# TensorE's transposes of gathered rows and of h's second half, set between the two groups of twelve second-layer products

## The chip, the cores and the metric

The kernel runs on one core of a Trainium2 chip. The metric is the device time of the program in microseconds (us), the median of three runs.

## What is computed

Attention over blocks of 64 positions (a query sees its own block and all before it), and then a mixture of experts that sends each token to one expert:

```python
# q, k, v: (8, 8, 576, 64);  w_gate: (512, 8);  w1: (8, 512, 1024);  w2: (8, 1024, 512)
scores = where(pos_i // 64 >= pos_j // 64, (q @ k.T) / 8, -1e9)
x = (softmax(scores) @ v)                    # reshaped to (4608, 512)
probs = softmax(x @ w_gate);  expert = argmax(x @ w_gate)
for e in range(8):
    mask = expert == e
    out[mask] = probs[mask, e] * (relu(x[mask] @ w1[e]) @ w2[e])
```

## The kernel before

Attention (class `Attention`) and routing (class `Router`) fill the first 372 us or so. Each token's row x is written to memory, and a table is built that lists the tokens of each expert in groups of 128, the tiles. The change concerns class `Experts`, which runs after that: 38 tiles, one after the other, each with its expert's weights.

Every product is made of three, since a float32 operand is split in a high and a low part: high times high, low times high, high times low. For one tile t:

- `gather(t)`: GpSimd issues an indirect DMA that fetches 128 rows into `xg`, two periods ahead.
- `rows_in(t)` (line 895): four TensorE transposes of `xg` into the bank `px`. `rows_act(t)` (lines 905 and 908): ScalarE copies it out twice, as the high part `xh` and whole as `xf`. `rows_pool(t)` (line 914): GpSimd makes the low part `xl` as their difference.
- `first_pe(t)` (line 936): 24 matmuls with w1; the halves f = 0 and 1 of the 1024 hidden values stand in two banks (`ph`, and one that the profile calls `o`). It starts with xh and needs xl from its fifth matmul on.
- The hidden values are transposed in two ways. Half 0: `planes` (line 983, ScalarE) takes `ph` apart in planes of 16 bits, `turned` (line 995) has the DMA transpose them from `h[0]` into `hf`, `joined` (line 1001) puts them together, and `joined_high` (lines 1009, 1010) applies the relu for the high part `hh` and for the whole. Half 1: `relu_act` (line 974), then `hidden_pe` (line 1018), four TensorE transposes into the bank `pt`, and `hidden_act` (lines 1028, 1031), two copies out of it.
- `hidden_low` (line 1037): GpSimd makes the low part `hl` of either half.
- `second_pe(t, part)` (line 1057): 24 matmuls with w2 into one bank, twelve in part 0 and twelve in part 1. Part 0 needs the high parts, and hl from its ninth matmul on.
- `out_act(t)` (line 1074) scales by the gate's weight, and `out_pool(t)` (line 1081) issues the DMA that scatters the rows.

The order on each engine is the order in which `period(t)` calls these; engines meet through semaphores. One call of `period(t)` holds the first layer of tile t, the rows of tile t + 1 and the second layer of tile t - 1. Some of the waits:

- `rows_act(t + 1)` waits for the rows' transposes, ScalarE's queue being strictly in this order;
- `hidden_pe(t, 1)` waits for both of ScalarE's steps that read the first layer's banks (`planes` and `relu_act(t, 1)`);
- `planes(t + 1)` writes `h[0]`, so it waits for the `hidden_low` of tile t that reads it; `relu_act` is behind it on ScalarE;
- `first_pe(t + 1)` waits for xh and, four matmuls on, for xl.

The weights of an expert (4 MB) come in eight DMAs issued by SyncE into five buffers (line 1176), and VectorE splits them (lines 1183, 1189) into one of two places, while the expert before is worked on. The first three tiles are special: their rows are fetched during attention, `begin()` handles tiles 0 and 1, and `period(2)` has the second layer of tile 0 and, before, another order.

Of the kernel before, what the change touches and what calls it, by code (L numbers as in the profile page):

```python
# [792 lines left out]
class Experts:  # L793
# [52 lines left out]
    def run(self):  # L846
# [37 lines left out]
        def gathered(t):  # L884

            return len([k for k in range(EARLY, t + 1) if k % 4 == t % 4])

        def rows_in(t):

            if t >= EARLY:  # L890
                pe.wait_ge(sg[t % 4], 16 * gathered(t))
            if t >= 2:
                pe.wait_ge(sem["xa"], 2 * t - 2)
            for k in range(4):
                m = pe.transpose(self.px[:, P * k : P * k + P], self.xg[t % 4][:, P * k : P * k + P], self.ident)
                if t == 1 and k < 2:

                    m.then_inc(sem[("mm1", "mm2")[k]], (3, 1)[k])
            m.then_inc(sem["xt"], 1)

        def rows_act(t):
            act.wait_ge(sem["xt"], t)
            if t >= 2:
                act.wait_ge(sem["mm1"], 2 * t + 1)
            act.copy(self.xh, self.px).then_inc(sem["xa"], 1)  # L905
            if t >= 2:
                act.wait_ge(sem["xp"], t - 1)
            act.copy(self.xf, self.px).then_inc(sem["xa"], 1)  # L908
# [59 lines left out]
        def relu_act(t, f):  # L968
            act.wait_ge(sem["mm1"], 2 * t + f + 2)
            if t == 2:  # L970
                act.wait_ge(sem["ht"], 4)
            elif t > 2:
                act.wait_ge(sem["hp"], 2 * t - 1)
            act.activation(self.h[f], self.ph[f], AF.Relu).then_inc(sem["ra"], 1)  # L974

        def planes(t):

            act.wait_ge(sem["mm1"], 2 * t + 2)
            if t == 2:
                act.wait_ge(sem["ht"], 3)  # L980
            else:
                act.wait_ge(sem["hp"], 2 * t)
            act.copy(  # L983
                self.h[0].bitcast(U16).rearrange("p (o c) -> p o c", o=2),
                self.ph[0].bitcast(U16).rearrange("p (c o) -> p o c", o=2),
            ).then_inc(sem["ra"], 1)

        def turned(t):

            if t == 2:  # L990
                act.wait_ge(sem["hp"], 4)
            else:
                act.wait_ge(sem["jo"], t - 2)
            act.wait_ge(sem["ra"], 2 * t - 1)
            act.dma_start_transpose(  # L995
                self.hf.bitcast(U16).rearrange("p (k c) -> p k c", c=P), self.h[0].bitcast(U16)
            ).then_inc(sem["tr"], 16)
# [14 lines left out]
        def hidden_pe(t, f):  # L1012
            if t:
                pe.wait_ge(sem["ra"], 2 * t + f - 1)
                pe.wait_ge(sem["ha"], 2 + 2 * f if t == 1 else 8 if t == 2 else 4 * t - 2)
            h = self.h[f] if t else self.xg[3 * f]
            for k in range(4):
                m = pe.transpose(self.pt[f][:, P * k : P * k + P], h[:, P * k : P * k + P], self.ident)  # L1018
            m.then_inc(sem["ht"], 1)

        def hidden_act(t, f):
            if t == 0 and f == 0:
                act.wait_ge(sem["lr"], 1)
                act.wait_ge(sem["lc"], 1)
            act.wait_ge(sem["ht"], 2 * t + f + 1 if t < 2 else t + 3)
            if t >= 2:
                act.wait_ge(sem["mm2"], t)
            act.copy(self.hh[t % 2][:, f], self.pt[f]).then_inc(sem["ha"], 1)
            if 0 < 2 * t + f < 4:
                act.wait_ge(sem["hp"], 2 * t + f)  # L1030
            act.copy(self.hf if t < 2 else self.h[f], self.pt[f]).then_inc(sem["ha"], 1)
# [7 lines left out]
        def second_pe(t, part):  # L1039
            e8, off = self.regs[t]  # L1040
            todo = [
                (h[t % 2], base, c) for h, base in ((self.hh, 8192), (self.hl, 8192), (self.hh, 12288)) for c in range(8)
            ]
            if part == 0:
                pe.wait_ge(sem["wh"], e8 + 8 if t >= EARLY else 4)
                pe.wait_ge(sem["ha"], 4 * t + 3)
                if t >= 2:
                    pe.wait_ge(sem["ya"], t - 1)
            for n in range(12 * part, 12 * part + 12):
                h, base, c = todo[n]  # L1050
                if n == 8:
                    pe.wait_ge(sem["hp"], 2 * t + 2)
                if t == 0 and n >= 16 and c % 2 == 0:
                    pe.wait_ge(sem["wd"], 5 + c // 2)
                elif n == 16:
                    pe.wait_ge(sem["wd"], e8 + 8)
                m = pe.matmul(  # L1057
                    self.py[t % 2],
                    h[:, c // 4, P * (c % 4) : P * (c % 4) + P],
                    wf[:, bass.ds(off + (base + 512 * c), 512)],  # L1060
                    start=n == 0,
                    stop=n == 23,
                )
            if part == 1:
                m.then_inc(sem["mm2"], 1)

        def out_act(t):
            act.wait_ge(sem["mm2"], t + 2)
            if t >= 1:
                act.wait_ge(sy, 16 * t)  # L1070
            else:

                act.wait_ge(sem["ga"], 48)
            act.activation(self.y, self.py[t % 2], AF.Copy, scale=self.xg[t % 4][:, GATE : GATE + 1]).then_inc(  # L1074
                sem["ya"], 1
            )
# [35 lines left out]
        def period(t):  # L1112
            more = t + 1 < NS
            if t > 2:
                first_pe(t)
                out_act(t - 2)
            planes(t)
            turned(t)
            relu_act(t, 1)
            if t == 2:  # L1120

                for f in range(2):
                    second_pe(0, f)
                out_act(0)
            elif more:
                rows_in(t + 1)
                rows_act(t + 1)
            hidden_pe(t, 1)
            hidden_act(t, 1)
            joined(t)  # L1130
            joined_high(t)
            for f in range(2):
                second_pe(t - 1, f)
                if t == 2 and f == 0:
                    rows_in(t + 1)
                    rows_act(t + 1)
            out_pool(t - 2)
            if t + 2 < NS:
                gather(t + 2)
            if more:  # L1140
                rows_pool(t + 1)
            for f in (1, 0):
                hidden_low(t, f, pool)
# [18 lines left out]
        with tc.tile_critical():  # L1162
# [94 lines left out]
            for t in range(2, least):  # L1257
                period(t)
# [135 lines left out]
```

## Time and profile before

| | |
|---|---|
| runs | 871.0, 877.45, 880.23 us; median 877.45 |
| profiled execution | 871.89 us, of which the span from first to last instruction is 870.1 |
| mean granted clock of TensorE | 0.987 of full |
| TensorE matmul busy | 825.4 us, 95% of the span |
| ScalarE, VectorE, GpSimd busy | 64%, 49%, 41% |
| second-layer matmuls (line 1057) | 912, 224.2 us busy |
| first-layer matmuls (line 936), halves 0 and 1 with xh | 280 each, 76.6 and 75.8 us |

The profile is of one execution. PE is TensorE's matmuls, PEld its loads of the stationary operand, which run ahead of them; DVE is VectorE, ACT ScalarE, POOL GpSimd, SP SyncE; a q behind a name is the engine's sequencer, which issues DMAs. A timeline row gives the start in us from the span's start, the duration, the engine, the line and operation, what is written and read, the count, and in brackets how long the engine had been idle and what ended that.

### The profile page before, as it was taken

The page shows a single profiled execution, that of the slowest core. Times are in us where ns is not written, and L with a number is a line of the kernel's source. Part 1 is how long each engine was busy: PE and PEld are TensorE (multiplying, and loading weights), DVE is VectorE, ACT ScalarE, POOL GpSimd, SP SyncE. Part 2 cuts the span into 40 slices and gives each one's busy share as a digit, 9 for nine tenths or more (in the row PEclk, how much of TensorE's full clock was granted, in tenths as well). Part 3 has the DMA queues.
Part 4 walks back from the last instruction along what each step waited for, and adds up shares of the span by engine and source line. Part 5 has one row for each costly group of instructions (what it writes and reads, how often), then busy time and mean ns, then how long its engine had stood idle before and what let it go on. Part 6 is the DMA issues. An engine that isn't in the chain of part 4 may idle for free.

```text
span 870.1 us, 16492 instructions
## 1 busy us (share of the span) xinstructions
PE 825.4 (95%) x5126; PEld 633.9 (73%) x5126; DVE 425.8 (49%) x1208; ACT 555.1 (64%) x1254; POOL 352.4 (41%) x390
## 2 busy tenths in 40 slices
PE   5999999999999999998998999998998799999997
PEld 4777767777777777676876877786777577777775
DVE  5778787878787877478034000158256343000000
ACT  6889888888888888444554455444544444555453
POOL 2000223232323412445554545456556355554453
PEclk8999999999999999999999999999999899999999
DMA  5234748363635353528427422259557752122222
GB/s 196 96 112 152 153 130 168 118 157 114 148 116 142 107 132 122 129 53 262 154 74 173 132 59 74 74 134 249 155 147 225 170 138 70 48 74 74 59 51 64
DMA packets 83707, 108.81 MB, mean 125 GB/s; under 512 B 45601, under 2 KB 48929, under 8 KB 83618
## 3 DMA queue, kind: packets, MB, share of 16 engines
q1 hardware_dynamic: 38082, 78.26, 31.3%
q0 software_dynamic: 7520, 19.97, 7.9%
q10 hardware_dynamic: 38016, 9.44, 6.7%
q8 instruction: 50, 0.82, 0.4%
q14 instruction: 39, 0.32, 0.1%
HBM read 76.76 MB, written 21.98 MB: 113 GB/s over the span
## 4 chain that ended last, share of the span: by engine, by line
PE 77%; issue 6%; ACT 6%; POOL 2%; DMA 2%; ACTq 1%; POOLq 1%; DVE 1%; DVEq 0%
PE py L1057 20%; PE o L304 10%; PE ph L936 10%; PE o L936 9%; PE o L339 4%; PE ya L202 3%; PE xa L202 3%; PE pt L1018 2%; ACT h L974 2%; PE yb L202 2%; DMA kd<-kT 2%; ACTq L995 1%; PE o L333 1%; POOLq L1079 1%; ACT pb L234 1%
## 5 line engine op out<-in xcount | busy, mean ns | idle before, releaser
L1057 PE MATMUL py<-w,low 128*128 (+1 forms) x912 | 224.2, 402 | 0.0
L1057 PEld LDWEIGHTS py<-w,low 128*128 128x128 f32 x912 | 171.0, 191 | 37.7 <-issue 0.3
L1183 DVE CAST w<-raw 128x1024 fp32r<-128x1024 f32 x60 | 50.0, 880 | 206.8 <-PE o L936 154.3
L1037 POOL TENSOR_TENSOR low<-h,low 128x512 fp32r<-128x512 f32 x72 | 105.6, 1468 | 62.9 <-ACT h L1010 62.5
L247 POOL TENSOR_SCALAR p<-p,rs 128x64 f32<-128x64 f32 x32 | 14.2, 443 | 257.2 <-DVE rs L243 154.8
L1189 DVE TENSOR_TENSOR w<-raw,w 128x1024 fp32r<-128x1024 f32 x60 | 87.2, 1510 | 0.0
L914 POOL TENSOR_TENSOR xl<-xf,xh 128x512 fp32r<-128x512 f32 x38 | 51.1, 1346 | 86.6 <-ACT xf L908 86.4
L983 ACT COPY h<-ph 128x1024 uint16<-128x1024 uint16 x36 | 36.5, 1013 | 69.8 <-PE ph L936 61.3
L936 PE MATMUL ph<-w,xh 128*128 x280 | 76.6, 396 | 2.1 <-ACT xh L905 2.1
L936 PE MATMUL o<-w,xh 128*128 x280 | 75.8, 393 | 0.0
L1001 ACT COPY h<-hf 128x1024 uint16<-128x1024 uint16 x36 | 43.0, 1193 | 48.7 <-DMA hf<-h 48.5
L1081 POOL DMA_INDIRECT out<-y,idx x35 | 42.7, 1220 | 63.3 <-ACT y L1074 52.1
L936 PEld LDWEIGHTS ph<-w,xh 128*128 128x128 f32 x280 | 53.1, 190 | 14.6 <-issue 2.5
L974 ACT ACTIVATE h<-o 128x512 f32<-128x512 f32 x37 | 22.1, 598 | 63.4 <-PE o L936 54.7
L1074 ACT ACTIVATE y<-py,xg 128x512 f32<-128x512 f32 x38 | 26.1, 686 | 56.0 <-PE py L1057 54.5
L936 PEld LDWEIGHTS o<-w,xh 128*128 128x128 f32 x280 | 52.7, 188 | 11.7
L234 ACT ACTIVATE pb<-ya,neg 128x320 f32<-128x320 f32 (+2 forms) x93 | 48.6, 533 | 2.5 <-PE pt30x L273 1.8
L234 ACT ACTIVATE pb<-yb,neg 128x320 f32<-128x320 f32 (+2 forms) x93 | 49.5, 547 | 0.0
L731 POOL DMA_INDIRECT tab<-toks,posi x40 | 41.7, 1042 | 15.1 <-issue 14.6
L1018 PE MATMUL pt<-ident,h 128*128 128x128 f32 x152 | 25.1, 290 | 23.1 <-ACT h L974 23.1
L339 PE MATMUL o<-fold,oT 128*128 128x144 f32 x256 | 45.4, 300 | 0.9 <-ACT oT L311 0.6
L219 DVE TENSOR_REDUCE neg<-ya 128x1 f32<-128x320 f32 (+2 forms) x93 | 44.8, 482 | 0.8 <-ACT pb L234 0.8
(965 smaller groups left out, 2137.7 us busy)
## 6 DMA issues: line engine op xcount, KB each, us to landing
raw<-w SPq DMA_DIRECT2D x60, 512.0 KB, 5.3
qd<-qT SPq DMA_DIRECT2D x32, 352.0 KB, 3.0
v<-vt SPq DMA_DIRECT2D x32, 352.0 KB, 4.7
kd<-kT SPq DMA_DIRECT2D x32, 288.0 KB, 3.4
xd<-xt SPq DMA_DIRECT2D x7, 1026.0 KB, 11.6
xd<-xg SPq DMA_DIRECT2D x9, 256.5 KB, 6.5
xg<-w SPq DMA_DIRECT2D x8, 256.0 KB, 6.2
xd<-x SPq DMA_DIRECT2D x8, 128.0 KB, 6.2
```

What stands on the lines that cost most here:

```text
L202: ins = mm(out, q[x][r, 128 * (i - 1) : 128 * i], q[y][r, o : o + w], start=n == 0, stop=n == 2, skip_group_check=True,)
L219: ins = self.nc.vector.tensor_reduce(self.neg[m][:, c : c + 1], src, AX.XY if i == 4 else AX.X, ALU.max, negate=True)
L234: ins = self.nc.scalar.activation(dst, src, AF.Exp, bias=self.neg[m][:, c : c + 1], scale=1.0, accum_out=self.sums[m][:, c : c + 1])
L304: self.nc.tensor.matmul(out[r], self.raws[m][2][:, slot], self.ph[m, bank][:, c0:c1], start=t in (0, 5), stop=t in (4, 5), skip_group_chec ...
L339: mm(t[:, i], self.oT[m, 0][:, o : o + P], w, start=True, stop=True)
L914: pool.tensor_sub(self.xl, self.xf, self.xh).then_inc(sem["xp"], 1)
L936: m = pe.matmul(self.ph[f], x[:, P * k : P * k + P], weights(k, f, part), start=start and k == 0, stop=stop and k == 3,)
L1001: act.copy(self.h[0].bitcast(U16).rearrange("p (c o) -> p c o", o=2), self.hf.bitcast(U16).rearrange("p (o c) -> p c o", o=2),).then_inc(s ...
L1037: engine.tensor_sub(hl, self.hf if t < 2 else self.h[f], hh).then_inc(sem["hp"], 1)
L1057: m = pe.matmul(self.py[t % 2], h[:, c // 4, P * (c % 4) : P * (c % 4) + P], wf[:, bass.ds(off + (base + 512 * c), 512)], start=n == 0, st ...
L1183: dve.tensor_copy(hi, raw[m % nr]).then_inc(sem["wh"], 1)
L1189: dve.tensor_sub(lo, raw[m % nr], hi).then_inc(sem["wd"], 1)
```

## The change

`period(t)` now has the first twelve second-layer products of tile t - 1 straight behind the first layer, ahead of the two groups of transposes, and the other twelve behind these:

```diff
@@ period(t)
             if t == 2:
                 for f in range(2):
                     second_pe(0, f)
                 out_act(0)
-            elif more:
+            second_pe(t - 1, 0)
+            if more:
                 rows_in(t + 1)
                 rows_act(t + 1)
             hidden_pe(t, 1)
             hidden_act(t, 1)
             joined(t)
             joined_high(t)
-            for f in range(2):
-                second_pe(t - 1, f)
-                if t == 2 and f == 0:
-                    rows_in(t + 1)
-                    rows_act(t + 1)
+            second_pe(t - 1, 1)
             out_pool(t - 2)
```

No instruction is added or removed, and no wait is. On ScalarE, VectorE and GpSimd the order stays the same from the period t = 3 on; only what ScalarE waits for in its second place (the rows' transposes) comes later in TensorE's order.

TensorE in a period from the fourth tile on, before, from the end of the first layer to the next tile's register loads (`px` and `pt` are the banks of the rows' and of h's transposes, `py_5896` the second layer's; low_75 and low_77 hold the high and the low part of the hidden values):

```order
L936 MATMUL o<-w,xh 128x512
L895 MATMUL px<-ident,xg_193 128x128 x4
L1018 MATMUL pt_5895<-ident,h_5890 128x128 x4
L1057 MATMUL py_5896<-w,low_75 128x512 x8
L1057 MATMUL py_5896<-w,low_77 128x512 x8
L1057 MATMUL py_5896<-w,low_75 128x512 x8
L923 TENSOR_LOAD e_207
```

The same place now:

```order
L936 MATMUL o<-w,xh 128x512
L1057 MATMUL py_5896<-w,low_75 128x512 x8
L1057 MATMUL py_5896<-w,low_77 128x512 x4
L895 MATMUL px<-ident,xg_193 128x128 x4
L1018 MATMUL pt_5895<-ident,h_5890 128x128 x4
L1057 MATMUL py_5896<-w,low_77 128x512 x4
L1057 MATMUL py_5896<-w,low_75 128x512 x8
L923 TENSOR_LOAD e_207
```

Eight products with the high part and four with the low part moved ahead of the transposes.

ScalarE in the period t = 2 before, behind the DMA transpose of tile 2:

```order
L974 ACTIVATE h_5890<-o 128x512
L1074 ACTIVATE y<-py_5896,xg_193 128x512
L1028 CAST low_75<-pt_5895 128x512
L1031 COPY h_5890<-pt_5895 128x512
L1001 COPY h_5889<-hf 128x1024
L1009 ACTIVATE low_75<-h_5889 128x512
L1010 ACTIVATE h_5889<-h_5889 128x512
L905 CAST xh<-px 128x512
L908 COPY xf<-px 128x512
```

And now:

```order
L974 ACTIVATE h_5890<-o 128x512
L1074 ACTIVATE y<-py_5896,xg_193 128x512
L905 CAST xh<-px 128x512
L908 COPY xf<-px 128x512
L1028 CAST low_75<-pt_5895 128x512
L1031 COPY h_5890<-pt_5895 128x512
L1001 COPY h_5889<-hf 128x1024
L1009 ACTIVATE low_75<-h_5889 128x512
L1010 ACTIVATE h_5889<-h_5889 128x512
```

The two copies of tile 3's rows (lines 905, 908) moved from behind the join of tile 2's hidden values to the front of these steps.

## The prediction

> **What bounds the kernel now.** I read the page first.
>
> ```profile
> PE 825.4 (95%) x5126; PEld 633.9 (73%) x5126; DVE 425.8 (49%) x1208; ACT 555.1 (64%) x1254; POOL 352.4 (41%) x390
> ```
>
> TensorE is busy 95% of the span, so a gain can only come from TensorE's idle time or from a clock below full. Attention lies before 372 us and is not touched. From there I went to the list of waits, for 400 to 870 us (total, times, longest).
>
> ```profile
> PEld pt L1018 <- ACT h L974: 30.4, 35, 5.6
> ACT h L1001 <- DMA hf<-h: 48.5, 15, 8.7
> ```
>
> The weight loads (PEld) of the transposes of h (L1018) wait 35 times for the relu of the second half (L974): 30.4 us. The timeline of one regular period (417.63 is its start T, 430.06 the next) shows what lies around that wait.
>
> ```profile
> 417.63 0.89 PEld L936 LDWEIGHTS ph<-w,xh 128*128 128x128 f32 x4
> ...
> 420.82 1.01 ACT L983 COPY h<-ph 128x1024 uint16<-128x1024 uint16 x1 [2.07 <-PE ph L936]
> 421.92 1.25 ACTq L995 DMA_TRANSPOSE hf<-h  x1
> 423.14 0.59 PEld L895 LDWEIGHTS px<-ident,xg 128*128 128x128 f32 x4
> 423.56 0.60 ACT L974 ACTIVATE h<-o 128x512 f32<-128x512 f32 x1 [1.73 <-PE o L936]
> 424.06 0.58 ACT L905 CAST xh<-px 128x512 fp32r<-128x512 f32 x1
> 424.21 0.42 PEld L1018 LDWEIGHTS pt<-ident,h 128*128 128x128 f32 x4 [0.49 <-ACT h L974]
> 424.60 5.41 PEld L1057 LDWEIGHTS py<-w,low 128*128 128x128 f32 x24
> 425.21 1.30 POOL L914 TENSOR_TENSOR xl<-xf,xh 128x512 fp32r<-128x512 f32 x1 [2.17 <-ACT xf L908]
> 426.42 1.17 ACT L1001 COPY h<-hf 128x1024 uint16<-128x1024 uint16 x1 [0.31 <-DMA hf<-h]
> 427.62 0.63 ACT L1009 ACTIVATE low<-h 128x512 fp32r<-128x512 f32 x1
> 428.16 0.61 ACT L1010 ACTIVATE h<-h 128x512 f32<-128x512 f32 x1
> 428.86 1.32 POOL L1037 TENSOR_TENSOR low<-h,low 128x512 fp32r<-128x512 f32 x1 [1.09 <-ACT h L1010]
> 430.06 0.88 PEld L936 LDWEIGHTS ph<-w,xh 128*128 128x128 f32 x4
> ```
>
> A period is 12.43 us. TensorE goes through 24 first-layer products, the row transposes (L895, T+5.5), a 0.49 us hole, the h transposes (T+6.6) and 24 second-layer products. The hole is the relu, which can only follow the last first-layer product.
>
> **The steady period after the change.** Twelve second-layer products, 24 of which take 5.41 us to load, come between the first layer and the rows: 2.7 us that need only what the previous period made. The rows start at T+8.2 or so, the h transposes at T+8.8; the relu ended at T+6.5, so the hole goes. 12.43 less 0.5 gives 11.9. From the fourth tile on there are 34 such periods (35 waits, the first of them counted with the start below): **17 us**.
>
> What is late next? Behind the rows, ScalarE's xh, xf, the two copies from pt, L1001, L1009 and L1010 all move 2.7 us. xh would end near T+9.7, xl (3.4 us from L895's start to L914's end now, part of it behind the relu) at T+11.6. The next period starts at T+11.9 and wants xl four products later, T+12.8: covered with 1.2 us to spare. L1037's end, now T+12.6, moves to about T+14.8, which is 2.9 us into the next period; L983 there waits for it and starts at 3.2 anyway. From L983's start to the relu's end are at most 3.3 us; the h transposes now want that only at T+8.8. So the loop of L983, DMA transpose, L1001, L1010 and L1037 may come about 2.5 us later than its place in a period before TensorE sees it; now it has about 0.3. On GpSimd the next period's output rows and gather stand behind L1037, on ScalarE its output scaling (L1074) behind L1010: they are issued up to 2 us later than now, the gather wanted 2.7 us later, and the scaling frees a bank that is written again only a period and a half on. SyncE's queue, which loads weights, is not passed by anything that moves.
>
> Splitting the products costs nothing by rows of the start, where one tile has that order already:
>
> ```profile
> 392.38 1.46 ACTq L995 DMA_TRANSPOSE hf<-h  x1
> 394.58 0.42 PEld L1018 LDWEIGHTS pt<-ident,h 128*128 128x128 f32 x4 [1.43 <-ACT h L974]
> 394.97 2.62 PEld L1057 LDWEIGHTS py<-w,low 128*128 128x128 f32 x12
> 397.63 0.59 PEld L895 LDWEIGHTS px<-ident,xg 128*128 128x128 f32 x4
> 398.19 2.63 PEld L1057 LDWEIGHTS py<-w,low 128*128 128x128 f32 x12
> 400.17 1.18 ACT L1001 COPY h<-hf 128x1024 uint16<-128x1024 uint16 x1 [3.81 <-DMA hf<-h]
> 402.43 0.57 ACT L905 CAST xh<-px 128x512 fp32r<-128x512 f32 x1
> 403.34 0.77 PEld L936 LDWEIGHTS ph<-w,xh 128*128 128x128 f32 x4 [2.52 <-issue]
> ```
>
> The rows (L895) follow twelve products without a hole, and twelve more follow them.
>
> **The start (t = 2).** Here ScalarE's order changes too: rows_act(3) goes ahead of the copies from pt and of L1001. Now L905 stands in the queue behind L1001, which waits 3.81 us for the DMA; TensorE gets xh at 403 and idles 2.52 us. After: the twelve products run from 393.15 (instead of a 1.43 us wait for the relu, late behind the DMA issue at 392.38), rows 395.8, h transposes 396.3, twelve products from 396.7, xh ready at 397.3, so the first layer of tile 3 begins at 399.4 instead of 403.34, and a regular period of 11.9 behind it puts the fourth tile's start at 411.3. Now that start is 417.63, 14.3 us after 403.34, since this period also waits for xl and runs slowly behind the idle time. **6 us**, this period's hole within it.
>
> **Late DMA transposes.** The landing time of L995's transposes, two L1037 in a row while VectorE split weights, and the rows around 570 to 600 and 680 to 690 us:
>
> ```profile
> DMA to landing us min/median/max: 3.1/4.0/12.9
> 566.20 3.99 POOL L1037 TENSOR_TENSOR low<-h,low 128x512 fp32r<-128x512 f32 x2
> 573.96 1.49 ACTq L995 DMA_TRANSPOSE hf<-h  x1
> 583.60 1.18 ACT L1001 COPY h<-hf 128x1024 uint16<-128x1024 uint16 x1 [5.45 <-DMA hf<-h]
> 589.64 1.25 ACTq L995 DMA_TRANSPOSE hf<-h  x1
> 591.64 0.42 PEld L1018 LDWEIGHTS pt<-ident,h 128*128 128x128 f32 x4 [3.46 <-ACT h L974]
> 597.68 1.18 ACT L1001 COPY h<-hf 128x1024 uint16<-128x1024 uint16 x1 [4.15 <-DMA hf<-h]
> 680.46 1.17 ACT L1001 COPY h<-hf 128x1024 uint16<-128x1024 uint16 x1 [8.70 <-DMA hf<-h]
> 687.72 0.71 PEld L1018 LDWEIGHTS pt<-ident,h 128*128 128x128 f32 x4 [5.61 <-ACT h L974]
> ```
>
> While an expert's weights stream in, a transpose lands after 9.6 us (573.96 to 583.60), 8.0 (589.64 to 597.68) or 12.9, and the next period's relu is late. Of the 30.4 us, 35 times 0.49 is 17.2; the other **13.2 us** are this: 3.0 and 5.1 in the two rows, 5.1 in all the rest. I work the new price with the loop: L983 to DMA issue 1.1, landing D, then 3.8 from L1001's start to L1037's end (426.42 to 430.18 above), 4.8 with the slower L1037. It takes 4.9 + D, or 5.9 + D while VectorE splits weights (two L1037 took 3.99 us there instead of 2.6; the second is behind the landing), against a period of 11.9; what is above that adds to L983's lateness, and 2.5 us of it are free. D of 12.9: 6.2 over, 3.7 us left (was 5.1). D of 9.6 and 8.0 in a row: 3.7 and 2.1 over, 3.3 left (was 3.0; a shorter period absorbs less). The rest fall mostly under the 2.5: I leave 1.4. 8.4 instead of 13.2: **5 us**, with bounds from a 3 us loss (the two bursts grow as D would let them if the traffic bunches up) to all 13.
>
> Those waits have a second price, in a table of stretches (PE busy, PEld, DVE, ACT, POOL, clock, DMA share, GB/s):
>
> ```profile
> 430.03:442.44 12.41, 12.16 (x57) 9.83 (x56) 0.00 (x0) 6.46 (x10) 6.20 (x7) 1.00 0.23 65
> 582.08:599.01 16.93, 13.71 (x57) 10.97 (x56) 14.05 (x15) 7.77 (x12) 8.67 (x6) 0.90 0.75 161
> 648.92:663.24 14.32, 12.23 (x57) 9.88 (x56) 11.91 (x12) 8.74 (x13) 8.03 (x6) 1.00 0.61 176
> 675.67:695.12 19.45, 13.97 (x57) 11.02 (x56) 7.13 (x8) 8.87 (x13) 7.15 (x7) 0.82 0.71 180
> ```
>
> After the two long waits the granted clock is 0.90 and 0.82 in the mean of the stretch, and the same 57 matmuls and transposes keep TensorE busy 13.71 and 13.97 us instead of 12.16: 3.4 us together. The stretch from 648.92, 1.9 us over a regular period by such a wait, keeps 1.00. After the change the first burst's 3.3 us fall in two periods (1.2 and 2.1), so one wait that costs clock is left, the 3.7: **1.4 us** saved (between 0 and 3.4). [...]
>
> **The end.** Before, the last 24 products follow at once:
>
> ```profile
> 855.13 0.63 ACT L1009 ACTIVATE low<-h 128x512 fp32r<-128x512 f32 x1
> 858.00 5.41 PEld L1057 LDWEIGHTS py<-w,low 128*128 128x128 f32 x24 [0.26 <-issue]
> ```
>
> L1009 ends 2.2 us ahead of them. It moves 2.7 later and they move 0.5 earlier, so they wait about 1 us: **0.9 lost**.
>
> **Sum.** 17 + 6 + 5 + 1.4 - 0.9 = 28.5 us. The profiled execution took 871.89, which gives 843.4. It is at the fast end of the runs (871.0 to 880.2, median 877.45); off the median it would be 849. I take the middle, **846**.
>
> **Rivals.**
> 1. *The late transposes keep or raise their price*, because the chain that follows a landing is later in every period. Only the hole and the start are gained: 871.9 - 17 - 6 + 0.9 = 850, with the 3 us loss and the median's offset 853 to 858. For it: D comes from traffic that stays. Against: the free 2.5 us. 15%.
> 2. *A new wait takes the hole's place*: xl late at the fifth first-layer product. L914 took 1.3 us here, and L1037, the same kind and size, about 2 while VectorE split weights. If L914 took 2 in every period and stood 0.9 us longer in its queue, the wait would be 0.4 us: 14 of the 17 back, 857 to 863. Against: 1.2 us spare. 7%.
> 3. *Slower: the loop through the DMA transpose becomes the bound.* ScalarE and GpSimd issue closer together, and the transposes queue behind gather and output rows in every period. 4.9 + D beats 11.9 from D = 7.0, and beats the old 12.43 from 7.5. At D = 8.0 a period is 12.9: 34 x 0.5 - 6 + 0.9 = 12 us slower, 884; from a mean D of 7.9 it is beyond 1%. The median D of 4.0 speaks against it. 4%. [...]
> 4. *All late waits vanish*: another 8 us and 1 to 2 of clock, 833 to 838. 6%.
>
> My forecast, 839 to 852, has 68%. The range for 8 in 10 reaches into both neighbours: **835 to 860**. A measurement here tells about 1% (8.8 us) from no change: faster 0.88, same 0.07, slower 0.05.
>
> **What would show it.** Right: the L974 entry at L1018 gone or under 5 us; a regular period of 11.9; L905 at t = 2 before L1001 and the fourth tile's start near 411; L1001 rarely waiting, since it comes later. Wrong: a wait of L936 for xl or xh in every period; L983 waiting for L1037 by over 2.5 us outside the weight streams; a transposes' median landing well over 4.

## The result and the profile after

| | before | change |
|---|---|---|
| runs | 871.0, 874.62, 877.45, 880.23 us | 834.95, 835.86, 836.52, 839.05 us |
| median | 876.04 | 836.19 |
| profiled execution, span | 871.89, 870.1 | 834.95, 833.2 |
| TensorE's mean clock | 0.987 | 0.995 |

Executions of one kernel differ by up to some 2.5%, so the ratios here and below compare only those within 1.5% of the kernel's fastest, and can differ from the ratio of the medians. The ratio is 0.9552, interval 0.9494 to 0.961: 4.5% faster. Forecast was 846, range 835 to 860. The time lies in the range, but near its fast end: about 40 us were gained between the medians, and 36.9 between the two spans, where the sum had 28.5.

The page of the change, first part (busy time, share, instructions), and its list of waits for 365 to 840 us (total, times, longest), cut to the entries that matter:

```profile
PE 812.3 (97%) x5126; PEld 631.0 (76%) x5126; DVE 420.5 (50%) x1208; ACT 554.4 (67%) x1254; POOL 355.4 (43%) x390
```

```profile
ACT h L983 <- POOL low L1037: 21.4, 13, 2.6
...
ACT h L1001 <- DMA hf<-h: 4.0, 3, 2.8
...
PEld py L1057 <- issue: 1.2, 1, 1.2
PE py L1057 <- ACT low L1009: 0.8, 1, 0.8
PEld ph L936 <- POOL xl L914: 0.7, 1, 0.7
```

TensorE's instructions are the same in number and it is busy 13 us less; its share rises from 95% to 97%. Some 5 of the 13 us, by estimate, are products at half clock behind the long waits of before: the granted clock was 0.50 from 404.42 to 407.84, 592.16 to 595.57 and 684.32 to 691.14, and of the 9.9 us that TensorE was busy there about half would be left at full clock. Most of the rest is in the regular periods, 12.16 us before and 11.95 now for the same work; why the profile books 0.2 us less in a period without a hole was not looked into. The entry of the h transposes (L1018) waiting for the relu (L974), 30.4 us before, is not there any more. Nor is most of ScalarE's wait for the DMA transposes (L1001: 48.5 before, 4.0 now). ScalarE waits for something else instead: L983 for L1037, 13 times, at most 2.6 us. From the rows of tile 3 on, TensorE still waits 0.7 us at the start (for xl) and 1.2 at the end.

The timeline of a regular period of the change (795.36 to 807.32; start, duration, engine, line and operation, in brackets the idle time before and what ended it):

```profile
795.36 0.88 PEld L936 LDWEIGHTS ph<-w,xh 128*128 128x128 f32 x4
...
798.52 1.01 ACT L983 COPY h<-ph 128x1024 uint16<-128x1024 uint16 x1 [1.08 <-PE ph L936]
...
800.85 2.75 PEld L1057 LDWEIGHTS py<-w,low 128*128 128x128 f32 x12
...
803.64 0.59 PEld L895 LDWEIGHTS px<-ident,xg 128*128 128x128 f32 x4
804.20 0.47 PEld L1018 LDWEIGHTS pt<-ident,h 128*128 128x128 f32 x4
804.51 0.59 ACT L905 CAST xh<-px 128x512 fp32r<-128x512 f32 x1 [2.63 <-PE px L895]
...
805.66 1.29 POOL L914 TENSOR_TENSOR xl<-xf,xh 128x512 fp32r<-128x512 f32 x1 [3.85 <-ACT xf L908]
806.42 1.21 ACT L1001 COPY h<-hf 128x1024 uint16<-128x1024 uint16 x1
807.32 0.88 PEld L936 LDWEIGHTS ph<-w,xh 128*128 128x128 f32 x4
...
808.90 1.31 POOL L1037 TENSOR_TENSOR low<-h,low 128x512 fp32r<-128x512 f32 x1 [0.68 <-ACT h L1010]
```

From T = 795.36, the rows are at T+8.28 and the h transposes at T+8.84, without a bracket, so TensorE did not idle ahead of either. xl (L914) ends at T+11.6, L1037 at T+14.85, the next period begins at T+11.96. Those are the forecast's 8.2, 8.8, 11.6, 14.8 and 11.9. L1001 has no idle time before it: ScalarE comes to it later than the transpose lands.

Where the gain lies is best seen from three marks. The rows' transposes begin at the same time in both, and the last second-layer products end the work; the rows of the two lines in either kernel (count, shortest, median and longest in ns, first and last start), before and then after:

```profile
L895 PEld LDWEIGHTS px<-ident,xg x152: 137/140/143, 372.8 to 851.3; 128*128 128x128 f32 x152
L1057 PEld LDWEIGHTS py<-w,low x912: 186/188/337, 387.7 to 863.2; 128*128 128x128 f32 x183
```

```profile
L895 PEld LDWEIGHTS px<-ident,xg x152: 137/140/146, 373.0 to 816.0; 128*128 128x128 f32 x152
L1057 PEld LDWEIGHTS py<-w,low x912: 186/188/192, 387.9 to 825.7; 128*128 128x128 f32 x183
```

From the first to the last of these starts I speak below of the **expert stage**: 863.2 - 372.8 = 490.4 us before, 452.7 after. It leaves out the attention, which takes up to 9 us longer in some executions of the experiments and which none of them touches. The longest of the second-layer loads fell from 337 to 192 ns, and the granted clock of the change is at no point of the stage below full (1.00 from 373.0 to 825.7). Except for the change, which has two traces, a stage below is that of one trace.

- *To the first layer of tile 4 (the forecast's fourth tile; tiles count from 0):* 417.63 before, 412.34 after, 5.3 us.
- *The 33 periods from there to the start of the last one:* 427.6 us before, 395.0 after, 32.65 us. A regular period went from 12.43 to 11.95, which makes 33 x 0.48 = 15.8. The other 16.8 us lay above the regular period before and do not any more: by the forecast's rows they are 13.2 us of late transposes and 3.4 of slow clock, 16.6 together. Only 0.6 us above the regular period are left.
- *The last period and the end:* 24.8 before, 25.9 after, 1.0 us lost: 0.4 up to the last product's start, and 0.65 behind it, where no edit was made.

-5.3 - 32.65 + 1.0 = -36.9, the difference of the spans. One period of the change with much DMA traffic (columns: length; busy us and count of PE, PEld, DVE, ACT, POOL; clock; DMA share; GB/s) shows that the late transposes cost nothing there:

```profile
555.93:567.90 11.97, 11.97 (x58) 9.87 (x57) 3.25 (x2) 6.23 (x11) 8.27 (x7) 1.00 0.82 218
```

With 82% of the DMA engines busy the period is as long as without weights, and the clock is full. The landing times of the DMA transposes (L995) in the change:

```profile
DMA to landing us min/median/max: 3.2/4.1/9.3
```

The longest, 9.3, belongs to the first of them (t = 2); of those from t = 3 on none took over 6.3 us, where before six took 8 to 12.9 while weights came in. The forecast had left them as they were.

### The profile page after: what moved, and what is told of

Read it like the earlier page. It is cut to its first block, busy times and chain, and to the rows that moved or that the text cites. A ratio compares the mean times of both kernels' runs of the same rounds, so it can differ in the third digit from the quotient of the medians.

```text
span 833.2 us, 16492 instructions
## 1 busy us (share of the span) xinstructions
PE 812.3 (97%) x5126; PEld 631.0 (76%) x5126; DVE 420.5 (50%) x1208; ACT 554.4 (67%) x1254; POOL 355.4 (43%) x390
## 4 chain that ended last, share of the span: by engine, by line
PE 89%; DVE 2%; POOL 2%; ACT 2%; issue 1%; DMA 0%; ACTq 0%; POOLq 0%; DVEq 0%
PE py L1057 23%; PE o L936 12%; PE ph L936 12%; PE o L304 11%; PE o L339 4%; PE ya L202 4%; PE xa L202 3%; PE yb L202 2%; PE px L895 2%; PE pt L1018 2%; PE o L333 1%; ACT pb L234 1%; PE o L190 1%; DVE neg L219 1%; DVE w L1186 1%
## 5 line engine op out<-in xcount | busy, mean ns | idle before, releaser
L1057 PE MATMUL py<-w,low 128*128 (+1 forms) x912 | 226.9, 398 | 0.8 <-ACT low L1009 0.8
L1057 PEld LDWEIGHTS py<-w,low 128*128 128x128 f32 x912 | 168.8, 188 | 38.1 <-issue 1.2
L1180 DVE CAST w<-raw 128x1024 fp32r<-128x1024 f32 x60 | 48.1, 849 | 179.6 <-PE o L936 128.1
L247 POOL TENSOR_SCALAR p<-p,rs 128x64 f32<-128x64 f32 x32 | 14.2, 445 | 257.2 <-DVE rs L243 154.9
L1037 POOL TENSOR_TENSOR low<-h,low 128x512 fp32r<-128x512 f32 x72 | 107.1, 1491 | 21.2 <-ACT h L1010 21.0
L914 POOL TENSOR_TENSOR xl<-xf,xh 128x512 fp32r<-128x512 f32 x38 | 52.0, 1369 | 110.7 <-ACT xf L908 110.6
L1186 DVE TENSOR_TENSOR w<-raw,w 128x1024 fp32r<-128x1024 f32 x60 | 83.9, 1455 | 0.0
L905 ACT CAST xh<-px 128x512 fp32r<-128x512 f32 x38 | 22.3, 588 | 90.9 <-PE px L895 90.9
L983 ACT COPY h<-ph 128x1024 uint16<-128x1024 uint16 x36 | 36.4, 1012 | 45.3 <-PE ph L936 24.0
L974 ACT ACTIVATE h<-o 128x512 f32<-128x512 f32 x37 | 22.2, 600 | 61.8 <-PE o L936 48.2
L936 PEld LDWEIGHTS ph<-w,xh 128*128 128x128 f32 x280 | 52.6, 188 | 11.9
L1081 POOL DMA_INDIRECT out<-y,idx x35 | 38.0, 1085 | 41.0 <-issue 36.8
L877 POOL DMA_INDIRECT xg<-xd,idx x37 | 45.1, 1220 | 10.4 <-POOL idx L873 10.4
L1001 ACT COPY h<-hf 128x1024 uint16<-128x1024 uint16 x36 | 43.3, 1203 | 4.1 <-DMA hf<-h 4.0
```

Source lines behind the costliest of these rows:

```text
L877: pool.indirect_dma_start(out=self.xg[i], out_offset=None, in_=self.xd[:, :], in_offset=bass.IndirectOffsetOnAxis(ap=self.idx[:, t : t + 1 ...
L914: pool.tensor_sub(self.xl, self.xf, self.xh).then_inc(sem["xp"], 1)
L936: m = pe.matmul(self.ph[f], x[:, P * k : P * k + P], weights(k, f, part), start=start and k == 0, stop=stop and k == 3,)
L1037: engine.tensor_sub(hl, self.hf if t < 2 else self.h[f], hh).then_inc(sem["hp"], 1)
L1057: m = pe.matmul(self.py[t % 2], h[:, c // 4, P * (c % 4) : P * (c % 4) + P], wf[:, bass.ds(off + (base + 512 * c), 512)], start=n == 0, st ...
L1180: dve.tensor_copy(hi, raw[m % nr]).then_inc(sem["wh"], 1)
```

## The experiments

Two theories of the 16.8 us. **S, slack**: the new order lets the relu come about 2.5 us later before TensorE waits, and that is enough for all. **P, phase**: the landings themselves became shorter, because the work of VectorE and GpSimd and with it the weight loads now fall elsewhere in the period than the DMA transposes. The rows where VectorE splits weights for the first time after 440 us, before (its period starts at T = 442.47) and after (T = 436.22):

```profile
448.40 3.61 DVE L1183 CAST w<-raw 128x1024 fp32r<-128x1024 f32 x4 [35.04 <-PE o L936]
...
450.04 1.42 POOL L914 TENSOR_TENSOR xl<-xf,xh 128x512 fp32r<-128x512 f32 x1 [3.18 <-ACT xf L908]
...
451.42 4.02 POOL L1037 TENSOR_TENSOR low<-h,low 128x512 fp32r<-128x512 f32 x2
...
454.46 4.86 SPq L1176 DMA_DIRECT2D raw<-w  x4
...
459.23 2.45 ACTq L995 DMA_TRANSPOSE hf<-h  x1
```

```profile
442.16 2.50 DVE L1180 CAST w<-raw 128x1024 fp32r<-128x1024 f32 x4 [28.04 <-PE o L936]
...
444.58 6.83 DVE L1186 TENSOR_TENSOR w<-raw,w 128x1024 fp32r<-128x1024 f32 x4
...
445.99 5.95 SPq L1173 DMA_DIRECT2D raw<-w  x4
...
446.55 1.54 POOL L914 TENSOR_TENSOR xl<-xf,xh 128x512 fp32r<-128x512 f32 x1 [3.57 <-ACT xf L908]
...
448.04 4.54 POOL L1037 TENSOR_TENSOR low<-h,low 128x512 fp32r<-128x512 f32 x2
...
452.67 1.01 ACT L983 COPY h<-ph 128x1024 uint16<-128x1024 uint16 x1 [2.40 <-POOL low L1037]
...
453.77 1.25 ACTq L995 DMA_TRANSPOSE hf<-h  x1
```

VectorE starts at the same point in both (T+5.9), when the first layer has let go of its weights. Before, GpSimd's subtractions (L914, L1037) begin 1.6 us into VectorE's four casts, and these take 3.61 us; after, they begin 2.8 us later in the period, the casts take 2.50, and the first two of VectorE's four subtractions (L1189 before, L1186 after) take 1.21 us each, where the first two took 2.33 beside GpSimd's before. So the four loads that wait for these buffers leave at T+12.0, 14.2, 15.4 and 16.5 before, and at T+9.8, 10.9, 13.1 and 15.4 after. The transpose is issued at T+16.8 before, 0.3 us behind the last load, and at T+17.6 after, 2.2 us behind it, since L983 waited for L1037 here. It landed after 10.4 us before and after 5.5 now.

All experiments, with the kernel before run beside each series (medians 883.42, 879.79 and 881.0):

| | time, median (lowest to highest) | ratio to before (interval) | expert stage, first to last start |
|---|---|---|---|
| e1 h transposes only | 843.94 (840.67 to 849.63) | 0.9553 (0.9476 to 0.9631) | 375.9 to 835.1: 459.2 |
| e2 before, light loads | 863.17 (860.69 to 867.62) | 0.9779 (0.9708 to 0.985) | 377.6 to 852.0: 474.4 |
| e3 change, light loads | 842.66 (838.64 to 854.33) | 0.9519 (0.9429 to 0.9609) | 378.8 to 831.5: 452.7 |
| e4 change, GpSimd early | 863.74 (862.87 to 872.15) | 0.980 (0.972 to 0.9881) | 376.3 to 853.7: 477.4 |
| e5 cut at 4 | 848.32 (846.36 to 850.46) | 0.9638 (0.9579 to 0.9696) | 380.0 to 837.8: 457.8 |
| e6 cut at 20 | 868.76 (864.47 to 873.73) | 0.9845 (0.9782 to 0.9908) | 381.4 to 865.2: 483.8 |
| e7 cut at 8 | 850.77 (842.52 to 854.28) | 0.9634 (0.9552 to 0.9716) | 382.0 to 842.8: 460.8 |
| e8 e4 with light loads | 852.52 (850.81 to 857.46) | 0.969 (0.9624 to 0.9756) | 378.9 to 843.1: 464.2 |
| e9 change again | 839.9 (836.88 to 841.73) | 0.9567 (0.9507 to 0.9627) | 374.9 to 827.4: 452.5 |
| e10 start only | 879.95 (865.2 to 885.42) | 0.9958 (0.9875 to 1.0041) | 375.9 to 871.8: 495.9 |
| e11 before, narrow subtractions | 871.72 (864.31 to 878.05) | 0.9961 (0.989 to 1.0031) | 375.6 to 855.7: 480.1 |
| e12 change, loads held back | 840.5 (839.98 to 841.48) | 0.957 (0.9511 to 0.963) | 375.6 to 830.6: 455.0 |

**e1: only the h transposes between the groups.** From t = 3 on the rows' transposes stay straight behind the first layer.

```diff
-            second_pe(t - 1, 0)
+            if t == 2:
+                second_pe(t - 1, 0)
             if more:
                 rows_in(t + 1)
                 rows_act(t + 1)
+            if t > 2:
+                second_pe(t - 1, 0)
             hidden_pe(t, 1)
```

> From the fourth tile on only the h transposes go between the two groups of twelve; the rows' transposes stay straight behind the first layer, and t = 2 is as in the change. The hole before L1018 should go with this move alone: a regular period of 11.9 us. Theory S (the new order lets a late DMA transpose pass, some 2.5 us of lateness being free): the landings are as late as before the change (up to 10 or 13 us), and still 836 to 841 us. Theory P (GpSimd's subtractions moved out of the way of VectorE's splitting, so the weight loads leave earlier and the transposes no longer queue behind four of them): xl meets the four casts here as before, so some landings of 6 to 9 us come back, though few waits of TensorE; 836 to 843.

The hole goes here too (period 11.95). But xl keeps its old place, the four casts take 3.6 us again, the loads leave at T+10.9 to 16.5 with the transpose at T+16.4, and landings of 8.3 and 9.2 us are back, and 8.0 and 8.6 later (here from the issue to the start of L1001, which waited for them). Its list of waits:

```profile
ACT h L1001 <- DMA hf<-h: 19.0, 8, 4.1
PEld pt L1018 <- ACT h L974: 3.8, 3, 2.2
```

TensorE sees 3.8 us of them. So S holds for most of it: a pair of landings of 9.6 and 8.0 us led to 3.0 us of waiting before (3.46 less the hole), and one of 9.2 and 8.0 to 2.2 here. It does not hold for all, and no landing here is as long as the 12.9 of before. The expert stage is 6.5 us longer than the change's; 3.9 of that is the start (told under the start, below), the rest these waits.

**e2 and e3: the price of the weight traffic in either order.** From a point of the stream on, 16 of 128 partitions are loaded, an eighth of the bytes in the same number of DMAs; the weights are incomplete from there.

```diff
-                sp.dma_start(dst, self.chunk(row, c)).then_inc(sraw[m % nr], 16)
+                src = self.chunk(row, c)
+                if m >= 4 + nr:
+                    dst, src = dst[0:16], src[0:16]
+                sp.dma_start(dst, src).then_inc(sraw[m % nr], 16)
```

> The kernel before, with 7/8 of the bytes of the weight loads left out from the sixth load after the first four on (16 of 128 partitions are fetched; the sums are those of stale weights). Both theories: transposes land after about 4 us in all periods, the waits of 0.2 to 5.1 us and the slow stretches behind them go, 13 + 3 us, so 856 to 860 with a regular period of 12.4. If the late relu came from the engines and not from the DMA traffic: 868 or more.

> The changed kernel with the same bytes left out (sums of stale weights). If the change took the whole price of the traffic away, within 1.5 us of the changed kernel (834 to 837); if it only hides part of it, faster by what is left: 828 to 833.

```profile
PEld pt L1018 <- ACT h L974: 19.0, 36, 1.5
```

Before, the hole stays (that row, of e2) and 490.4 becomes 474.4: 16.0 us is what the traffic cost in one piece, against 13.2 + 3.4 from the profile. In the change the same edit takes nothing away, 452.7 and 452.7: by these traces the traffic is free in the new order. Both medians lie above what was expected (856 to 860 and 834 to 837); in the profiled executions the stage began 4.8 and 5.8 us later, which is attention.

**e4 and e8: GpSimd's work early again.** Two idle subtractions of 128x512 in each period, into a part of a buffer that nobody reads, start as soon as the first layer has ended, where GpSimd's own work now does not stand. e8 is the same with light loads, as in e3.

```diff
             gather(t + 2)
+            if t > 2:
+                pool.wait_ge(sem["mm1"], 2 * t + 3)
+                for j in range(2):
+                    pool.wait_ge(sem["ex"], 2 * (t - 3) + j)
+                    pool.tensor_sub(
+                        self.high[:, 2048:2560], self.high[:, 0:512], self.high[:, 512:1024]
+                    ).then_inc(sem["ex"], 1)
```

> The changed kernel with two more GpSimd subtractions of 128x512 in each period from t = 3, right behind the first layer, where the kernel before had xl and the low part (they write columns that nothing reads). Theory P: VectorE's four casts behind the first layer take about 3.6 instead of 2.5 us, the first weight load leaves 1 to 2 us later, and landings of 8 to 10 us come back in two or three periods, with 1 to 4 us of waits at L1018 in all: 836 to 842. Theory S alone: landings stay at 6.3 or less, as in the changed kernel, and the time within 1.5 us of it.

> The kernel of the two additional GpSimd subtractions, which took 477.4 us in the expert stage, with 7/8 of the bytes of the weight loads left out as in the light kernels (sums of stale weights). If its loss of 24.8 us came by the landings of the DMA transposes, they fall back to 4 to 6 us and the stage to 453 to 456. If it came by GpSimd's time itself (xl and the low parts late wherever VectorE splits weights), the stage stays above 465.

The waits of e4, its row of landing times, and then the waits of e8:

```profile
ACT h L1001 <- DMA hf<-h: 40.2, 13, 6.9
ACT h L983 <- POOL low L1037: 35.6, 19, 4.0
PEld ph L936 <- POOL xl L914: 13.4, 14, 3.1
PEld pt L1018 <- ACT h L974: 8.9, 6, 1.7
```

```profile
DMA to landing us min/median/max: 4.0/4.4/11.0
```

```profile
ACT h L983 <- POOL low L1037: 51.1, 18, 4.1
...
PEld ph L936 <- POOL xl L914: 14.2, 14, 2.8
```

e4 costs 24.8 us against the change, far more than I had expected of it. The four casts take 5.0 us, more than the 3.6 of before, so e4 puts back more than the change had taken away. Long landings are back (8.9 to 11 us, in the groups where the last load leaves beside a transpose), as P says, and 13.3 of the 24.8 us go with the traffic (477.4 to 464.2). The other 11.5 stay in e8, where a landing holds ScalarE up only once, at t = 2: GpSimd itself is late with xl and the low parts. I had set the two causes against each other, 453 to 456 or above 465; it was both.

**e5, e7, e6: four, eight and twenty products ahead of the transposes instead of twelve** (from t = 3 on). The edit, with `cut` 4, 8 or 20:

```diff
-        def second_pe(t, part):
+        def second_pe(t, part, cut=12):
...
-            for n in range(12 * part, 12 * part + 12):
+            for n in range(*((0, cut), (cut, 24))[part]):
...
-            second_pe(t - 1, 0)
+            second_pe(t - 1, 0, 4 if t > 2 else 12)
...
-            second_pe(t - 1, 1)
+            second_pe(t - 1, 1, 4 if t > 2 else 12)
```

> The changed kernel with the cut after 4 second-layer products instead of 12 from t = 3 on. Four products take 0.9 us, more than the hole of 0.5, so a regular period is 11.95 us as in the change. xl moves to T+8.5, behind VectorE's four casts but into its first subtraction. Theory P (the phase of GpSimd's and VectorE's work sets how late a transpose lands): some landings of 7 to 9 us come back; with only 0.7 us of lateness free here, 2 to 6 us of waits: expert stage (first rows' transposes to last product) 454 to 459 us against 452.6 in the change. Theory S alone (free lateness, landings as before the change): 13 us less about 0.5 per late period, 460 to 464.

With four, the hole is gone as well and landings of 7.5, 8.9 and 8.1 come back, which cost

```profile
PEld pt L1018 <- ACT h L974: 4.2, 4, 1.4
```

The last load and the next transpose are at T+16.5 and T+16.4. The stage is as expected, and the start makes 3.8 of the 5.1 us against the change.

> The changed kernel with the cut after 8 products from t = 3 on. The last tile's chain ends 0.9 us earlier than with 12, so its wait before the last 24 products shrinks from 1.4 to 0.5 us; lateness free is 1.6 us. Theory P: xl at T+9.4 touches the end of VectorE's first subtraction in two or three periods, landings up to 7 us, no wait or under 1 us: expert stage 451.5 to 453.5.

With eight I expected the change's stage within a microsecond or so, and found 8.1 us more: a miss. One landing of 10.1 us made most of it. The last of its four loads left at T+16.6, the transpose at T+16.5; the rows of what follows:

```profile
464.11 1.25 ACTq L995 DMA_TRANSPOSE hf<-h  x1
...
476.70 3.55 POOL L1037 TENSOR_TENSOR low<-h,low 128x512 fp32r<-128x512 f32 x1 [5.09 <-ACT h L1010]
...
481.44 1.25 ACTq L995 DMA_TRANSPOSE hf<-h  x1
483.44 0.68 PEld L1018 LDWEIGHTS pt<-ident,h 128*128 128x128 f32 x4 [3.85 <-ACT h L974]
```

and that stretch among the windows (columns as above):

```profile
471.00:488.40 17.40, 13.79 (x58) 11.11 (x57) 7.04 (x8) 7.22 (x11) 8.93 (x7) 0.90 0.78 198
```

L1037, late behind the landing, falls among VectorE's subtractions and takes 3.55 us instead of 1.3; L983 waits for it, the relu is behind L983, TensorE idles 3.85 us, and the clock of that stretch is 0.90. One such chain makes a period of 17.4 instead of 11.95: 5.4 of the 8.1 us, the start most of the rest. It is a wait of the kind that the forecast kept in the change, 3.7 us with a slow clock behind it. The forecast's loop, 5.9 + 10.1 us against 11.95 with 1.6 us free at eight products, gives 2.5; the slower L1037 is the rest. Two landings of 8.3 us in this trace cost 0.45 us each. The change had no landing of such a length.

> The changed kernel with the cut after 20 products from t = 3 on. xl ends at about T+13.5 and the next period wants it at T+12.9: a new wait of 0.6 us in each of 34 periods takes the hole's place, the prediction's second rival. Expert stage 470 to 477 us, regular period 12.5 to 12.6, and the waits of the first layer for xl in every period.

```profile
PEld ph L936 <- POOL xl L914: 31.0, 35, 3.6
```

With twenty, xl is late in every period and the period 12.5, as expected; this is the forecast's second rival, made real. The stage was 7 us over the expected range. Against the change, the start is 5.5 us longer (xl came 3.6 us late there), the 33 periods 21.7, with about 1 us more in some where weights are split, and the end 4.0.

**e9: the change once more.** No edit; a second trace of it.

> The changed kernel once more, beside the other three on one chip, since attention takes some us longer on some chips than in the first profiles. Theory P: the last of four weight loads leaves about 2 us ahead of the next DMA transpose, as in the first profile; landings stay at 6.5 or less from the fourth tile on, no wait at L1018, expert stage 452 to 455 us.

The stage is 452.5, no wait at L1018, and no landing over 7.0 us after t = 2, where I had expected 6.5. The result does not hang on one execution.

**e10: the start alone.** Only the order of t = 2, all later periods as before (against the kernel before).

```diff
                 out_act(0)
-            elif more:
+                second_pe(t - 1, 0)
+            if more:
                 rows_in(t + 1)
...
-            for f in range(2):
-                second_pe(t - 1, f)
-                if t == 2 and f == 0:
-                    rows_in(t + 1)
-                    rows_act(t + 1)
+            if t > 2:
+                second_pe(t - 1, 0)
+            second_pe(t - 1, 1)
```

> The kernel before with the new order in the period t = 2 alone. The fourth tile starts 4 to 6 us earlier; from there on as before the change, holes of 0.49 and late landings included: expert stage 483 to 487 us against 490.4. If the start's gain were lost again in the later periods, 489 or more.

0.9958 with an interval on both sides of 1: inconclusive. In its one trace the stage is 495.9, where I had expected 483 to 487: a miss. I had said 489 or more if the gain were lost again in later periods, but the start itself did not have it. The wait

```profile
PEld ph L936 <- POOL xl L914: 4.1, 1, 4.1
```

lies in tile 3's first layer and ate the start's gain: tile 4 began 1.3 us later than before, counted from the first rows. The 33 periods from there took 431.2 us, 3.5 more than before in the same order, with one landing of 14.2; that is how far two traces of one order can lie apart. The start is not shown alone.

**e11: before, with GpSimd's subtractions out of VectorE's way.** They cover 64 of 512 columns from tile 4 on (the low parts are incomplete).

```diff
-            pool.tensor_sub(self.xl, self.xf, self.xh).then_inc(sem["xp"], 1)
+            c = slice(0, 512 if t < 4 else 64)
+            pool.tensor_sub(self.xl[:, c], self.xf[:, c], self.xh[:, c]).then_inc(sem["xp"], 1)
...
-            engine.tensor_sub(hl, self.hf if t < 2 else self.h[f], hh).then_inc(sem["hp"], 1)
+            c = slice(0, 512 if t < 4 else 64)
+            engine.tensor_sub(hl[:, c], (self.hf if t < 2 else self.h[f])[:, c], hh[:, c]).then_inc(sem["hp"], 1)
```

> The kernel before with GpSimd's subtractions (xl and the low parts of the hidden values) cut from 512 to 64 columns from tile 4 on; the other columns keep old values, so the sums differ. Theory P: nothing holds VectorE's splitting up, the four loads leave 2 to 3 us earlier (the last at T+13 to 14 instead of 16.5, the transpose at T+16.7), landings fall from 8 to 13 us to 6.5 or less, and the waits above the hole go, 16 us, without any change of order: stage 472 to 476. If the landings do not depend on that phase, they stay at 8 or more, and the loop, 1 us shorter, still makes 5 to 10 us of waits: 480 to 486.

The same place as in the two fences above, with T = 446.7; lines from 914 on are one or more higher here:

```profile
452.67 2.62 DVE L1185 CAST w<-raw 128x1024 fp32r<-128x1024 f32 x4 [35.10 <-PE o L937]
...
454.31 0.43 POOL L915 TENSOR_TENSOR xl<-xf,xh 128x64 fp32r<-128x64 f32 x1 [3.18 <-ACT xf L908]
...
455.22 4.88 DVE L1191 TENSOR_TENSOR w<-raw,w 128x1024 fp32r<-128x1024 f32 x4
...
456.63 4.00 SPq L1178 DMA_DIRECT2D raw<-w  x4
...
463.49 1.29 ACTq L996 DMA_TRANSPOSE hf<-h  x1
```

and TensorE's wait for the relu in its list of waits:

```profile
PEld pt L1019 <- ACT h L975: 21.5, 36, 3.4
```

In the order of before, with GpSimd brief, the casts take 2.62 us, the last load leaves 3.2 us ahead of the transpose, and landings of 10.4, 9.6 and 9.1 in these groups become 4.2 to 4.9. This shows P's first link, from GpSimd's work to the landings, without touching TensorE's order. What it is worth is less clear, since brief subtractions also shorten the loop behind a landing. The 33 periods became 12.1 us shorter, of 16.8. The stage falls only to 480.1, 4 us short of what I had expected under P and at the edge of what I had expected without it, and the whole time is not measurably different: one landing of 11.5 us stays, in another group, where four loads leave at T+3.6 to 7.4 around a transpose at T+4.3, and costs the 3.4 us at the end of that row and slow clock (the 24 second-layer loads behind it take 6.97 us instead of 5.42); and the start was 1.5 us later.

**e12: the change with its loads held back.** SyncE waits for a small DMA ahead of each load, which was to bring the loads next to the transposes again.

```diff
                         sp.wait_ge(sem["wd"], m)
+                    if m >= 9:
+                        sp.dma_start(self.pause, self.w1[0, 0:1, 0:8]).then_inc(sem["pa"], 16)
+                        sp.wait_ge(sem["pa"], 16 * (m - 8))
                     load(m, row)
```

> The changed kernel with a DMA of 32 bytes ahead of each weight load from the tenth on, which SyncE waits for, so that each load leaves some 2 us later and the last of four after the next DMA transpose's issue. Theory P: landings of 7 to 10 us come back in two or three periods without any change on GpSimd, VectorE or TensorE; the loop is 1 to 3 us late beyond what is free, so 1 to 4 us of waits: stage 453.5 to 457. If the weight loads' phase does not matter, landings stay at 6.5 or less and the stage within 1 us of the changed kernel's.

Right in its sum and wrong in its way. Most loads were held back by 3 to 4 us, so they left one at a time (T+11.2, 14.8, 18.7, 24.9 around a transpose at T+17.8), and no landing after t = 2 was over 6.6 us, where 7 to 10 were expected. A single load beside a transpose did not bring the long landings back. So the last link of P, from the loads' issue to the landings, has no experiment that moves the four loads together and nothing else. The 2.3 us of longer stage go with a period of 12.05 us instead of mostly 11.95; why it is longer is open.

What there is for this link is a comparison over the traces. Ahead of the transposes of tiles 7, 16 and 21, VectorE frees four buffers in a row in each of the kernels below. The table has how far from the transpose the last of the four loads is issued (- ahead of it, + behind) and the three landings, in us (e1's trace has no landing times, and in e12 the loads are spread):

| | last load | landings |
|---|---|---|
| e4 | +1.2 | 11.0, 8.9, 9.3 |
| e7 | +0.1 | 10.1, 8.3, 8.3 |
| e5 | +0.1 | 7.5, 8.9, 8.1 |
| before | -0.3, -0.2, -0.2 | 10.4, 9.6, 9.1 |
| e10 | -0.3, -0.2, -1.7 | 9.3, 8.9, 5.8 |
| change | -2.2 | 5.5, 5.8, 6.3 |
| e9 | -2.2 | 6.3, 6.5, 7.0 |
| e11 | -3.2 | 4.2, 4.8, 4.9 |
| e6 | -4.7 | 4.4, 4.4, 4.6 |

## Why the prediction was right, and where it fell short

- **The hole, 17 us: right.** 15.8 in 33 periods of 11.95, and one more period in the last stretch; the times within the period came as worked out. What was to be late next was covered: xl in all periods but one, L1037 by L983's wait of at most 2.6 us. e1, e5 and e7 show that twelve, four or eight products ahead of the h transposes close the hole, and e6 that the room behind it ends before 20.
- **The start, 6 us: 5.3, right in the change, but luck is part of it.** xh came in time, and xl 0.7 us late. In e1, e5 and e6, whose order up to there is the same, the fourth tile began at 416 to 418 (counted from the same first rows), with xl 3 to 4 us late. In e7, e8 and e10 it began at 414 to 419, and in e3, e4, e9 and e12 at 412 as in the change. One small copy of GpSimd ahead of a gather (L873, 128x1, near 386.5) goes with this: it takes 0.18 to 0.34 us in the five traces with the early start, where it begins ahead of a subtraction of VectorE, and 1.05 to 1.28 us in the six others, where the subtraction begins up to 0.2 us ahead of it or, in e10, 0.01 behind. What stands behind it on GpSimd came 2 to 4 us later in these. That the one makes all of the other was not tested. The change has the early start in both of its traces.
- **Late transposes, 5 of 13.2 us, and 1.4 of 3.4 us of clock: this step failed in its size.** The sum left 8.4 us of waits and one slow stretch, by taking the old landings D (12.9, 9.6, 8.0) into the new loop. (One term is off by the forecast's own rule: 5.9 + 12.9 is 6.9 us over 11.9, and 4.9 + 12.9 is 5.9, not 6.2.) All 16.8 us went. D itself changed: at most 6.3 us (7.0 in e9), and 4.9 + D or 5.9 + D then hardly exceeds the period, so the free 2.5 us cover it. What the sum lacked is that VectorE, GpSimd and SyncE's loads move against the transposes when the rows move: the prediction said that nothing passes SyncE's queue, which is true of its order and not of its times. Late landings that cost little (e1, e5) show that the free time is real, and e7 shows the chain of a long D. That the landings depend on when GpSimd works is shown from two sides, e4 (put back, landings of 9 to 11 us) and e11 (taken away before, 4.2 to 4.9). That it is the loads' issue which lengthens them rests on the comparison above, and how much of the 10.4 us beyond the forecast (16.8 less 5 and 1.4) is slack and how much is shorter landings was not separated.
- **The end, 0.9 lost: right.** The last 24 products wait 1.2 us, 0.3 before. Up to the last product's start the last stretch lost 0.4 us, as a hole of 0.5 less 0.9 makes; the other 0.65 came behind the last product and were not forecast.
- **The rivals.** The fourth, all late waits gone (833 to 838, 6%), is the one that came true, in the median too: 836.19 lies below the 839 to 852 that had 68%. So the range was right by its width, and not by the forecast's own course. Under the first rival the late waits would have stayed; e7 shows one of them. The second needed eight more products ahead (e6), and the third a D above 7 in every period: no experiment had it.

## What to carry to other kernels

When a step is moved, ask not only which wait goes but which transfers will start at another point of the period: here the late transposes were worth as much as the hole itself, and they went because they came earlier and because there was room behind them. A landing time read from the trace belongs to the order in which it was measured; if a sum for another order uses it, its range should reach to the undisturbed landing. A gain that rests on two streams just missing each other should be tried in neighbouring versions (here 4, 8, 12 and 20 products ahead), which tell how much of it is margin and how much is phase.

## What the runs showed of the hardware

From t = 3 on, in the ten traces with whole weight loads and landing times, a DMA transpose of 128x1024 elements of 16 bits landed after 3.1 to 6.1 us (median 4.1, 213 of them) when no weight load of 512 KB was issued within 5 us of it, and after at most 7.0 us with one or two loads there (43). All 25 landings over 7.4 us, up to 14.2, had three or four loads there. But so had 69 that took 3.2 to 7.3 us, so the bunch alone is not enough; what else decides is open.

A subtraction of VectorE (128x1024) took 1.21 us alone and 2.33 beside GpSimd's, and one of GpSimd (128x512) 1.3 alone and 2.3 beside VectorE's. Changing from products to transposes and back within an accumulation of 24 cost TensorE nothing that the rows show: 12.43 us less the hole of 0.49 is the new period.

Behind three idle times of TensorE's loads in before the granted clock was 0.50: 2.52 us (until 403.34, the row in the forecast; 0.50 from 404.42 to 407.84), 3.46 us (until 591.64; from 592.16 to 595.57) and 5.61 us (until 687.72; here from 684.32, within the idle time, to 691.14). In e7 the stretch of 17.4 us with 3.85 us of idle time had a clock of 0.90 in the mean, and in e11 the 24 loads behind 3.41 us took 6.97 us instead of 5.42. But 2.22 and 2.32 us in before (until 476.68 and 657.37) were followed by a clock of 1.00, and behind 2.90 us in e7 (until 412.57) four first-layer loads took 0.88 us, as at full clock. So 2.52 us cost clock once and 2.90 us did not: in these traces the length of an idle time alone does not tell whether clock is lost.
